# An attention and mixture-of-experts kernel: keys of unit 0 ahead of its diagonals on GpSimd, its state update behind its y, two decay tables turned one unit earlier

## The chip, the cores and the metric

The kernel runs on one core of a Trainium2 chip. The metric is the device time of one execution in microseconds (us); smaller is better. The engines are TensorE (PE; its weight loads are shown apart as PEld), VectorE (DVE), ScalarE (ACT), GpSimd (POOL) and SyncE (SP), which here only issues DMA transfers. Each engine works through its own instructions in program order.

## The reference

An attention with a decaying state feeds two dense blocks. For batch b, head h and step t, with r, k, v of width 48 and per-head vectors w (decay) and u (bonus):

```
y[t]  = r[t] @ (state + outer(u * k[t], v[t]))
state = w * state + outer(k[t], v[t])
```

There are 4 batches, 8 heads and 768 steps, all in fp32. The y of all heads, laid out as 3072 tokens of 384 features, goes through a soft mixture of 8 experts with 4 slots each (a softmax over tokens to fill the slots, a two-layer expert, a softmax over slots to mix back), and then through a two-layer block of width 2048 with a leaky relu.

## The kernel before, in words

The attention works in 24 units: 6 chunks of 128 steps, and in each chunk 4 pairs of heads. Unit i belongs to chunk i // 4 and pair i % 4, and holds all 4 batches. Its data come in two transfers: rk (r and k with the features on the partitions, 512 KB) and tk (v, k and r with the steps on the partitions, 576 KB). Both have 5 buffers, so tk of unit i+5 can be fetched only when unit i has read its own for the last time. All transfers are issued on SP, in program order (load, L225).

For one unit, the steps and the engines they run on are:

- powers (L285): a table of powers of w for a pair, from scans on DVE, with copies on ACT. It is done once per pair, for the first four units only.
- powers_t (L293): turns that table with a PE transpose into PSUM (tile psE, pool psM, 2 buffers) and copies it on ACT into KH (L297).
- scale (L304): multiplies r and k of rk by the powers; the k half on DVE, the r half on POOL or, for units 3 to 6 and a few more, on DVE (L309).
- bonus (L311): r * u * k, two operations, on DVE for units 0 and 1 and on POOL after them (L315, L318).
- diag (L320): sums that product on DVE into Dg (L323) and spreads it into the diagonal of the tile base: on POOL by an affine_select for units 0 and 1 (L329), on ACT by 8 operations for the others (L338). base has 2 buffers.
- keys (L343): multiplies k of tk in place by KH, on POOL (L348).
- scores (L354): 8 products on PE of k and r into the PSUM tile A (L359), which has one buffer.
- keep (L364): copies the causal half of A over base, two operations on DVE (L367). It frees A for the scores of the next unit.
- attend (L375): y of the unit on PE, from base and v (L398) and, from chunk 1 on, from the state (L390).
- update (L403): 8 products on PE of the keys and v into the PSUM tile U of pool psM (L412), and one operation on DVE that puts U into the state St (L418 in chunk 0, L420 after it).
- evac (L424): copies y to SBUF on ACT (L431); logits and tokens (L433, L445) take it on to the mixture.

The loop over units (L568) writes the order of the work on every engine out by hand: unit i+4 is loaded, unit i+2 scaled, unit i+1 scored and kept, unit i attended. The steps of the first units stand ahead of the loop, with dummy products on PE (warmup, FILL) between them. The state of chunk 0 is first read by the attend of unit 4, so the updates of units 0 and 1 need not stand directly behind their y: in this kernel the update of unit 0 is issued at the end of turn 1, that of unit 1 in the middle of turn 2 (between the scores and the keep of unit 3), and from unit 2 on each stands at the end of its own turn. keys(0) is issued in turn 0, keys(1) at the end of turn 0, keys(2) at the end of turn 1. The transposes of tables 2 and 3 both stand at the end of turn 1.

After the attention come the experts, then the mixing and the first products of the last block, and from about 164 us to the end the long loop of the last block (L1028, L971).

Of the kernel before, what the change touches and what calls it, by code (L numbers as in the profile page):

```python
# [118 lines left out]
def chunked(ctx, tc, rk, tok, wT, urep, phi, w1, w2, w2f, win, wout, outT, dbg=None, check=False):  # L119
# [35 lines left out]
    def load_w2_unit(j):  # L155
        t = ld.tile([128, 3 * DM], F32, name=f"w2t{j}", tag="tk")
        load_w2(t, 5 * j, 3)
        load_w2(rkf[(NU - NLD + j) % NLD].rearrange("p a b c -> p (a b c)"), 5 * j + 3, 2)
# [12 lines left out]
    def narrow_b(t, k, out=None):  # L171
        lo = t[:, k, 0]
        nc.vector.tensor_scalar(
            lo if out is None else out, lo.bitcast(U32), 2.0**-29, 7.0, op0=ALU.mult, op1=ALU.min
        )
# [117 lines left out]
    def powers_t(hp):  # L293
        e = ex[:, hp, :]
        ps = psM.tile([128, 128], F32, name=f"psE{hp}", tag="m")
        nc.tensor.transpose(ps[:, 0:R], e[:, C : 2 * C], ident[:R, :R])
        nc.scalar.copy(  # L297
            KH[:, hp, :].rearrange("p (h d) -> p h d", h=2),
            ps.rearrange("p (h d) -> p h d", h=2)[:, :, 0:D],
        )  # L300
# [3 lines left out]
    def scale(i, eng=nc.gpsimd, part=(0, 1)):  # L304
        for x in part:
            t = rk_t[i][:, x]
            e = ETp[:R] if (x or i in SCALE_V) and i else ET
            e = e[:, i % NP : i % NP + 1, :].broadcast_to([R, B, C])
            (nc.vector if x or i in SCALE_V else eng).tensor_tensor(t, t, e, op=ALU.mult)  # L309

    def bonus(i, eng=nc.gpsimd):  # L311
        hp = i % NP
        kk = tk_t[i][:, 1]
        rr = tk_t[i][:, 2]
        eng.tensor_tensor(  # L315
            rr, rr, u_sb[:, hp : hp + 1, :].broadcast_to([128, B, 2 * D]), op=ALU.mult
        )
        eng.tensor_tensor(rr, rr, kk, op=ALU.mult)  # L318

    def diag(i):  # L320
        rr = tk_t[i][:, 2]
        Dg[i] = sm.tile([128, 2 * B], F32, name=f"Dg{i}", tag="Dg")
        nc.vector.tensor_reduce(  # L323
            Dg[i].rearrange("p (h b) -> p b h", h=2),
            rr.rearrange("p b (h d) -> p b h d", h=2), op=ALU.add, axis=AX.X,
        )
        base[i] = bp.tile([128, 2, B, C], F32, name=f"base{i}", tag="base")
        if i in AFFINE:
            nc.gpsimd.affine_select(  # L329
                out=base[i].rearrange("p a b c -> p (a b) c"),  # L330
                in_=Dg[i].unsqueeze(2).broadcast_to([128, 2 * B, C]),
                compare_op=ALU.is_equal, fill=0.0,
                base=-(C - 1), pattern=[[0, 2 * B], [1, C]], channel_multiplier=1,
            )
            return
        for b in range(B):
            for h in range(2):
                nc.scalar.activation(  # L338
                    base[i][:, h, b, :], anti, AF.Copy, scale=Dg[i][:, h * B + b : h * B + b + 1]
                )  # L340


    def keys(i, eng=nc.gpsimd):  # L343
        if i >= NU - NP:
            return
        hp = i % NP
        kk = tk_t[i][:, 1]
        eng.tensor_tensor(  # L348
            kk, kk, KH[:, hp : hp + 1, :].broadcast_to([128, B, 2 * D]), op=ALU.mult
        )  # L350
# [3 lines left out]
    def scores(i):  # L354
        a = apsum[i] = psA.tile([128, 2, B, C], F32, name=f"A{i}", tag="A")
        for b in range(B):
            for h in range(2):
                p0 = 64 * h
                nc.tensor.matmul(  # L359
                    a[:, h, b, :], rk_t[i][p0 : p0 + D, 1, b, :], rk_t[i][p0 : p0 + D, 0, b, :],  # L360
                    start=True, stop=True,
                )
# [40 lines left out]
    def update(i):  # L403
        c, hp = divmod(i, NP)
        if c < NC - 1:
            v = tk_t[i][:, 0]
            u = psM.tile([128, B, D], F32, name=f"U{i}", tag="m")
            kk = tk_t[i][:, 1]
            for b in range(B):
                for h in range(2):  # L410
                    n = D if h else 64
                    nc.tensor.matmul(  # L412
                        u[64 * h : 64 * h + n, b, :], kk[:, b, D * h : D * h + n],
                        v[:, b, D * h : D * h + D], start=True, stop=True,
                    )
            st = St[:, hp]
            if c == 0:
                nc.vector.tensor_copy(st, u[:R])  # L418
            else:
                nc.vector.scalar_tensor_tensor(  # L420
                    st, st, W128[:, hp : hp + 1], u[:R], op0=ALU.mult, op1=ALU.add
                )
# [114 lines left out]
    def load_weights(n):  # L537
        if n < WH:
            wirs[n] = wp.tile([128, WCW, 2], I32, name=f"wir{n}", tag="wt")
            load_wide(win[n], wirs[n])  # L540
        elif n < WH + 16:
            load_w1(n - WH)
        else:
            load_rows(n - WH - 16)
# [10 lines left out]
    powers(1)  # L555
    scale(0, nc.vector, part=(1, 0))
    bonus(0, nc.vector)
    diag(0)
    powers_t(0)
    scores(0)  # L560
    warmup(FILL[0])
    scale(1)
# [5 lines left out]
    for i in range(NU):  # L568
        c, k = divmod(i, NP)
        for n in range(len(WST)):  # L570
            if WST[n] == i:
                load_weights(n)
        if i + NLD - 1 < NU:
            load(i + NLD - 1)
        else:
            load_w2_unit(i + NLD - 1 - NU)
        if i + 2 < NU:
            scale(i + 2)
        for _ in range(FILL_L.get(i + 1, 0)):
            nc.tensor.matmul(  # L580
                lw[0].rearrange("p a t -> p (a t)")[:, C:], ident,
                u_sb.rearrange("p a d -> p (a d)"), start=False, stop=True, skip_group_check=True,
            )
        if i + 1 < NU:
            scores(i + 1)
            if i == 2:
                update(1)
            keep(i + 1)
        slot = bool(c) and k == 1
        if i >= 1 and not slot:  # L590
            logits(i - 1)
        if 2 <= i < NP:
            tokens(i - 2)(nc.scalar.copy)
        if i + 2 < NU:
            bonus(i + 2)
        if i == 0:
            keys(0)
        attend(i)
        if slot:
            soft2(c - 1)  # L600
        evac(i)
        if c and k == 0:
            soft1(c - 1)
        if i < 2:
            for hp in ((1,), (2, 3))[i]:
                powers_t(hp)
            keys(i + 1)
        if i == 0:
            powers(3)
        if i == 2:  # L610
            keys(3)
        if i == NP:
            nc.gpsimd.memset(ones, 1.0)
        if i == NU - 2:
            yps[NU - 1] = psE.tile([128, 4, C], F32, name="ylast", tag="E")
            nc.vector.memset(yps[NU - 1][32:64, 0:2], 0.0)
        if check and i == NU - 2:
            rc0 = ap.tile([R, NP], F32, name="rc0")
            nc.vector.tensor_single_scalar(rc0, w_sb, WLO, op=ALU.is_ge)
            nc.vector.scalar_tensor_tensor(rc0, w_sb, WHI, rc0, op0=ALU.is_le, op1=ALU.mult)  # L620
            nc.vector.tensor_reduce(mst[:R, 6:7], rc0, op=ALU.add, axis=AX.X)
            nc.vector.memset(mst[:R, 7:8], 1.0)
        if i + 2 < NU:
            diag(i + 2)
            if i + 2 >= NP:
                keys(i + 2)
        if i > 1:
            update(i)
        elif i == 1:
            update(0)  # L630
        if i >= NP - 1:
            tok_copy = tokens(i - 1)
        if slot:
            pS = slots(c - 1)
            logits(i - 1)
        if i >= NP - 1:
            tok_copy(nc.vector.tensor_copy if c and k == 0 else nc.scalar.copy)
        if slot:
            slots_add(c - 1, pS)
        if i in NARROW:  # L640
            j, x = divmod(NARROW.index(i), 2)
            w = slice(x * WCW // 2, (x + 1) * WCW // 2)
            low = psM.tile([128, WCW // 2], I32, name=f"low{i}", tag="m")
            narrow_b(wirs[j], w, low)
            narrow_c(wi[:, j, w], wirs[j], w, low)
            narrow_d(wi[:, j, w], wirs[j], w, low)
        if i in NARROW_A:
            j, x = divmod(NARROW.index(NARROW_A[i]), 2)
            w = slice(x * WCW // 2, (x + 1) * WCW // 2)
            narrow_a(wi[:, j, w], wirs[j], w)  # L650
# [557 lines left out]
```

## Time and profile before

| what | value |
|---|---|
| time, median of 3 runs | 387.8 us (386.18 to 390.62) |
| the profiled execution, its own time | 384.81 us |
| its span, first to last instruction | 383.1 us |
| mean granted TensorE clock | 0.994 |
| busy PE / DVE / ACT / POOL | 96% / 72% / 61% / 37% of the span |
| read from memory | 64.80 MB |

The shares are averages over stages with different limits. What the change touches lies in the first 30 us or so, where the first units start up; so the stretch of those units, engine by engine, is what has to be read. Times in the rows below are counted from the start of the span. A row of the timeline has the start, the duration, the engine, the line, the operation and, in brackets, how long the engine stood idle just before it and what ended that. Neighbours of one kind are merged, with their count behind an x.

### The profile page before, as it was taken

How to read it: one execution, taken by the hardware profiler on the slowest of the kernel's cores; microseconds unless marked ns; L12 is line 12 of the kernel's file. 1: busy time of each engine (PE TensorE's matmuls, PEld its weight loads, DVE VectorE, ACT ScalarE, POOL GpSimd, SP SyncE). 2: the span in 40 equal slices, each digit the busy share in tenths (PEclk: the TensorE clock that was granted, in tenths of full speed). 3: DMA queues.
4: the chain of work that ended last, by engine and by line, in shares of the span. 5: the costliest groups of instructions: out<-in, count | busy, mean ns of one | idle time of the engine just before them, and what ended most of it. 6: DMA issues, size and time to landing. Idle time of an engine off the chain costs nothing.

```text
span 383.1 us, 8324 instructions
## 1 busy us (share of the span) xinstructions
PE 366.6 (96%) x3160; PEld 283.1 (74%) x3160; DVE 274.7 (72%) x478; ACT 232.2 (61%) x541; POOL 141.7 (37%) x145
## 2 busy tenths in 40 slices
PE   6799999999989999899999999999999999999994
PEld 3478778788765346778888878888888888888883
DVE  6879998888986544877577755777766766586762
ACT  3379879888883133756775657677655455545540
POOL 4797889988614002155433312554200000000000
PEclk9899999999999999999999999999999999999999
DMA  7979999999999999300022220000000220021202
GB/s 244 395 266 417 415 415 414 416 418 411 417 418 407 420 426 421 154 2 0 0 86 82 83 84 0 1 2 1 2 2 0 82 84 0 1 99 67 82 3 90
DMA packets 18018, 70.16 MB, mean 183 GB/s; under 512 B 2240, under 2 KB 3248, under 8 KB 17840
## 3 DMA queue, kind: packets, MB, share of 16 engines
q1 hardware_dynamic: 17968, 69.53, 45.7%
q8 instruction: 27, 0.44, 0.5%
q14 instruction: 23, 0.19, 0.1%
HBM read 64.80 MB, written 4.72 MB: 181 GB/s over the span
## 4 chain that ended last, share of the span: by engine, by line
PE 85%; DVE 7%; ACT 3%; DMA 2%; issue 2%; SPq 1%; DVEq 0%; ACTq 0%
PE o L1028 49%; PE h L971 5%; PE A L359 5%; PE Y L398 5%; PE po L806 3%; PE ph L763 3%; PE Y L390 2%; PE U L412 2%; PE px L448 2%; DMA tk<-in_tok_dram 2%; PE l L440 2%; DVE base L367 2%; PE l L517 1%; DVE rkb L309 1%; DVE t L981 1%
## 5 line engine op out<-in xcount | busy, mean ns | idle before, releaser
L985 ACT CAST gh<-t 128x512 fp32r<-128x512 f32 x94 | 58.4, 621 | 70.4 <-DVE t L981 67.8
L981 DVE TENSOR_TENSOR t<-t,h 128x512 f32<-128x512 f32 (+1 forms) x97 | 65.6, 677 | 23.9 <-ACT t L977 23.2
L1028 PE MATMUL o<-gh,woh 128*128 128x512 f32 x279 | 80.1, 393 | 0.2 <-ACT woh L873 0.2
L1028 PE MATMUL o<-gl,woh 128*128 128x512 f32 x279 | 79.9, 392 | 0.0
L1028 PE MATMUL o<-gh,wol 128*128 128x512 f32 x279 | 79.8, 392 | 0.0
L990 DVE TENSOR_TENSOR gl<-t,gh 128x512 fp32r<-128x512 f32 x71 | 50.8, 715 | 39.8 <-ACT gh L985 39.8
L977 ACT ACTIVATE t<-h 128x512 f32<-128x512 f32 (+1 forms) x97 | 57.4, 593 | 10.2 <-PE h L971 10.1
L1028 PEld LDWEIGHTS o<-gh,woh 128*128 128x128 f32 x279 | 52.2, 188 | 12.2 <-ACT woh L873 0.7
L1028 PEld LDWEIGHTS o<-gh,wol 128*128 128x128 f32 x279 | 52.1, 188 | 12.0 <-issue 0.4
L1028 PEld LDWEIGHTS o<-gl,woh 128*128 128x128 f32 x279 | 52.4, 188 | 11.5
L338 ACT ACTIVATE base<-anti,Dg 128x128 f32<-128x128 f32 x176 | 53.9, 391 | 5.4 <-DVE Dg L323 5.3
L990 POOL TENSOR_TENSOR gl<-t,gh 128x512 fp32r<-128x512 f32 x23 | 34.5, 1498 | 58.5 <-ACT gh L985 47.0
L971 PE MATMUL h<-cT,Gs 128*128 128x512 f32 (+1 forms) x97 | 37.3, 390 | 1.4 <-ACT Gs L939 1.4
L367 DVE COPY_PREDICATED base<-mask,A 128x512 f32<-128x512 int32 x48 | 34.1, 734 | 5.1 <-ACT base L338 4.5
L359 PE MATMUL A<-rkb 48*128 48x128 f32 x384 | 28.2, 286 | 4.1 <-DVE ETw L275 1.7
L359 PEld LDWEIGHTS A<-rkb 48*128 48x128 f32 x384 | 23.7, 188 | 9.4 <-POOL rkb L309 1.9
L398 PE MATMUL Y<-base,tk 128*48 128x128 f32 x376 | 26.4, 284 | 0.0
L315 POOL TENSOR_TENSOR tk<-tk,u_sb 128x384 f32<-128x384 f32 x22 | 22.1, 1004 | 7.8 <-DMA tk<-in_tok_dram 6.1
L398 PEld LDWEIGHTS Y<-base,tk 128*48 128x48 f32 x376 | 20.1, 126 | 5.1 <-issue 3.0
L318 POOL TENSOR_TENSOR tk<-tk 128x384 f32<-128x384 f32 x22 | 22.2, 1008 | 1.7
L971 PEld LDWEIGHTS h<-cT,Gs 128*128 128x128 f32 x97 | 18.0, 188 | 5.7 <-ACT Gs L939 1.8
L309 DVE TENSOR_TENSOR rkb<-rkb,ETp 112x512 f32<-112x512 f32 x31 | 20.4, 680 | 1.2 <-DMA rkb<-in_rk_dram 0.7
(198 smaller groups left out, 467.8 us busy)
## 6 DMA issues: line engine op xcount, KB each, us to landing
tk<-in_tok_dram SPq DMA_DIRECT2D x23, 576.0 KB, 9.3
rkb<-in_rk_dram SPq DMA_DIRECT2D x24, 512.0 KB, 9.5
w<-in_w_dram SPq DMA_DIRECT2D x16, 768.0 KB, 11.2
wir<-in_win_dram SPq DMA_DIRECT2D x8, 768.0 KB, 13.2
w<-in_w2f_dram SPq DMA_DIRECT2D x8, 768.0 KB, 12.7
out_dram<-sum SPq DMA_DIRECT2D x17, 256.0 KB, 2.1
wor<-in_wout_dram SPq DMA_DIRECT2D x4, 768.0 KB, 14.7
wir<-in_wout_dram SPq DMA_DIRECT2D x4, 768.0 KB, 4.3
```

Source lines behind the costliest of these rows:

```text
L309: (nc.vector if x or i in SCALE_V else eng).tensor_tensor(t, t, e, op=ALU.mult)
L318: eng.tensor_tensor(rr, rr, kk, op=ALU.mult)
L338: nc.scalar.activation(base[i][:, h, b, :], anti, AF.Copy, scale=Dg[i][:, h * B + b : h * B + b + 1])
L359: nc.tensor.matmul(a[:, h, b, :], rk_t[i][p0 : p0 + D, 1, b, :], rk_t[i][p0 : p0 + D, 0, b, :], start=True, stop=True,)
L367: nc.vector.copy_predicated(base[i][:, :, 2 * j : 2 * j + 2, :], mask.unsqueeze(1).unsqueeze(1).broadcast_to([128, 2, 2, C]), a[:, :, 2 * ...
L398: nc.tensor.matmul(ys[r][g : g + D, j, :], v[:, b, D * h : D * h + D], base[i][:, h, b, :], start=c == 0, stop=True, skip_group_check=True,)
L971: nc.tensor.matmul(t, Gs[f // 8][:, f % 8 * 128 : f % 8 * 128 + 128], cT[blk // 3][:, blk % 3 * TB + c.start : blk % 3 * TB + c.stop], sta ...
L977: nc.scalar.mul(tt[n][:, c], t, 0.01)
L981: nc.vector.tensor_tensor(tt[n][:, c], tt[n][:, c], h, op=ALU.max)
L985: nc.scalar.copy(gh[n][:, c], tt[n][:, c])
L990: eng.tensor_tensor(gl[n][:, c], tt[n][:, c], gh[n][:, c].bitcast(F32), op=ALU.subtract)
L1028: nc.tensor.matmul(os[m][:, c], w[j][:, k, m * 128 : (m + 1) * 128], g[n][:, c], start=k == 0 and w is woh and g is gh and c.start == 0, s ...
```

## The change

keys(0), with powers_t(0) that it needs, moves from turn 0 of the loop to just ahead of diag(0); on POOL it then comes before the affine_select of unit 0 instead of behind the bonus of unit 2. Every update stands at the end of its own turn: that of unit 0 in turn 0, ahead of the scores of unit 2, that of unit 1 in turn 1, ahead of the scores of unit 3. The transpose of table 2 moves from turn 1 to turn 0. No operation is added or taken away.

```diff
     bonus(0, nc.vector)
+    powers_t(0)
+    keys(0)
     diag(0)
-    powers_t(0)
     scores(0)
...
         if i + 1 < NU:
             scores(i + 1)
-            if i == 2:
-                update(1)
             keep(i + 1)
...
-        if i == 0:
-            keys(0)
         attend(i)
...
         if i < 2:
-            for hp in ((1,), (2, 3))[i]:
+            for hp in ((1, 2), (3,))[i]:
                 powers_t(hp)
             keys(i + 1)
...
-        if i > 1:
-            update(i)
-        elif i == 1:
-            update(0)
+        update(i)
```

## Rows read from the trace of the kernel before

**Rows 1.** The page, chain that ended last, shares of the span by engine.
```profile
PE 85%; DVE 7%; ACT 3%; DMA 2%; issue 2%; SPq 1%; DVEq 0%; ACTq 0%
```

**Rows 2.** Chain of waits, 16 to 26 us: start, us, what.
```profile
16.20 1.46 PE A L359 x16
17.66 0.58 PE l L440 x8
18.24 1.88 PE Y L398 x16
20.12 0.46 PE psE L296 x2
20.58 0.42 issue
21.00 0.64 PE U L412 x14
...
22.48 1.09 PE A L359 x16
23.57 0.59 PE U L412 x14
24.17 0.36 PE l L440 x8
...
25.06 1.01 PE Y L398 x16
```

**Rows 3.** Busy time by stretch: window, length, engines, granted clock, DMA share, GB/s.
```profile
17.00:18.00 1.00, 1.00 (x15) 0.56 (x12) 0.92 (x2) 0.74 (x4) 1.00 (x3) 0.50 1.05 421
...
20.00:21.00 1.00, 0.58 (x4) 0.32 (x3) 0.73 (x1) 0.95 (x4) 0.99 (x2) 0.83 0.12 45
...
42.00:53.00 11.00, 10.15 (x191) 8.47 (x189) 10.46 (x22) 8.36 (x25) 8.77 (x10) 1.00 1.02 412
```

**Rows 4.** Timeline of PE, scores of units 1 and 2.
```profile
11.01 1.16 PE L359 MATMUL A<-rkb 48*128 48x128 f32 x16 [0.86 <-DVE base L367]
...
16.20 1.46 PE L359 MATMUL A<-rkb 48*128 48x128 f32 x16 [1.71 <-DVE ETw L275]
```

**Rows 5.** Timeline of ACT, 7 to 33 us.
```profile
7.18 0.24 ACT L297 COPY KH<-psE 128x96 f32<-128x96 f32 x1 [1.25 <-PE psE L296]
...
14.77 0.24 ACT L297 COPY KH<-psE 128x96 f32<-128x96 f32 x1
...
17.67 2.45 ACT L338 ACTIVATE base<-anti,Dg 128x128 f32<-128x128 f32 x8 [0.26 <-DVE Dg L323]
...
21.64 2.45 ACT L338 ACTIVATE base<-anti,Dg 128x128 f32<-128x128 f32 x8 [0.60 <-DVE Dg L323]
...
26.60 2.45 ACT L338 ACTIVATE base<-anti,Dg 128x128 f32<-128x128 f32 x8
...
30.34 2.45 ACT L338 ACTIVATE base<-anti,Dg 128x128 f32<-128x128 f32 x8
```

**Rows 6.** Timeline of DVE, 9 to 25 us.
```profile
9.43 1.32 DVE L367 COPY_PREDICATED base<-mask,A 128x512 f32<-128x512 int32 x2
11.06 0.56 DVE L315 TENSOR_TENSOR tk<-tk,u_sb 128x384 f32<-128x384 f32 x1 [0.31 <-DMA tk<-in_tok_dram]
...
20.15 0.73 DVE L367 COPY_PREDICATED base<-mask,A 128x512 f32<-128x512 int32 x1 [0.43 <-ACT base L338]
21.05 0.55 DVE L323 TENSOR_REDUCE Dg<-tk 128x8 f32<-128x384 f32 x1 [0.16 <-POOL tk L318]
...
24.22 0.36 DVE L418 COPY St<-U 112x192 f32<-112x192 f32 x1 [0.98 <-PE U L412]
```

**Rows 7.** Timeline of POOL, affine_select of unit 0; keys of units 0 and 1.
```profile
8.22 1.09 POOL L329 TENSOR_SCALAR_AFFINE_SELECT base<-Dg 128x1024 f32<-128x1024 f32 x1 [4.71 <-DVE Dg L323]
...
17.01 1.96 POOL L348 TENSOR_TENSOR tk<-tk,KH 128x384 f32<-128x384 f32 x2
```

**Rows 8.** Timeline of SP, the transfer tk of unit 5.
```profile
21.73 0.33 SPq L238 DMA_DIRECT2D tk<-in_tok_dram  x1
```

## The prediction

> **What bounds the kernel now.** I read the chain that ended last first: PE carries 85% of it [rows 1], and from 16.2 us on it is PE nearly without a break. No PE work is added or removed, so the change can only win what PE loses by waiting or by its clock while the first units start up. The chain of waits between 16 and 26 us [rows 2] shows what that is. PE stands 1.71 us idle before the scores of unit 2 at 16.20 us, which wait for the keep of unit 1 on DVE [rows 4]. After that the granted clock is 0.50 (1.2 GHz) from 17 us on and full again within 20 to 21 us [rows 3]. In that stretch scores, logits and attend take 1.46, 0.58 and 1.88 us where the same work takes 1.09, 0.36 and 1.01 us a few us later [rows 2]: 0.37 + 0.22 + 0.87 = 1.46 us are lost to the clock. Behind them stand two transposes (0.46 us), a wait of 0.42 us and the update of unit 0 (0.64 us), all at the end of turn 1, and the update of unit 1 (0.59 us) in turn 2.
>
> A second loop runs beside PE: ACT spreads the diagonals of a unit (2.45 us), DVE keeps the second half (0.73 us), reduces the next unit's diagonal (0.55 us), and ACT spreads again [rows 5, 6]. With the handovers that is about 3.75 us, and the spreads of units 4 and 5 already follow each other at 30.34 - 26.60 = 3.74 us [rows 5]. Between 42 and 53 us DVE is busy 10.46 of 11 us [rows 3]: there DVE is the bound, and what is won earlier survives only if DVE's own queue has come forward.
>
> **The change part by part.** All times are those of the profiled execution: span 383.1 us, time 384.81 us, so 1.71 us lie around the span. The median of the runs shown is 387.8 us, 2.99 us above it; I carry the difference over unchanged.
>
> *keys(0) ahead of the diagonals of unit 0, on POOL.* It needs KH of pair 0, ready at 7.18 + 0.24 = 7.42 us [rows 5], so it starts at about 7.55 us (an estimate) and takes half of the pair's 1.96 us, 0.98 us [rows 7]. Queued behind it on POOL is the affine_select of unit 0, which moves from 8.22 us to 8.55 us, 0.33 us later, and behind that the r half of scale(1). The keep of unit 0 waits for the affine_select and moves from 9.43 to 9.76 us, ending at 11.08 us instead of 10.75 us. The next DVE step, the bonus of unit 1, had stood 0.31 us idle for its transfer until 11.06 us [rows 6]; that idle time covers all but 0.02 us. If the transfer landed earlier the cover is gone and the cost is 0.33 us. I take 0.05 us. On PE the scores of unit 1 move from 11.01 to about 11.34 us; that is hidden, since PE idles before the scores of unit 2.
>
> *keys(0) gone from 17 us.* POOL runs without a pause there, so the bonus of unit 3 ends 0.98 us earlier, and the 0.16 us that DVE waits for it at 21.05 us go [rows 6, 7]. Next late is DVE itself, with the second half of the keep of unit 2.
>
> *Table 2 and update(0) in turn 0.* Both fall into the 1.71 us in which PE stood idle. The transpose costs 0.46 / 2 = 0.23 us at the low clock. update(0) takes the PSUM buffer of table 1, so it waits for that copy on ACT, which ended at 14.77 + 0.24 = 15.01 us [rows 5] and now ends near 15.34 us; with some 0.1 us of handover and 0.64 us of work [rows 2] it ends near 16.1 us. Queued behind it are the scores of unit 2, due at 16.20 us, so it costs nothing by 0.1 us; at worst, if the copy comes later, I give it 0.3 us. The state copy of unit 0 (0.36 us [rows 6]) goes in front of scale(3) on DVE, where the 0.43 us wait before the keep at 20.15 us [rows 6] covers it; uncovered it would cost 0.36 us.
>
> *What that takes out of turns 1 and 2.* On PE: one transpose, 0.23 us, the wait, 0.42 us, and one update, 0.59 us, together 1.24 us, whatever the clock does. If the clock stays full, another 1.46 us; PE alone could then be 2.7 us ahead at the scores of unit 4. On DVE, the state copy of unit 1 at 24.22 us had waited 0.98 us for PE with the keep of unit 3 queued behind it [rows 6]. After the change that copy comes before scale(4), and the keep of unit 3 starts as soon as its diagonals are spread.
>
> *The sum.* The ACT-DVE loop then decides. Its entry hardly moves: the spread of unit 2 at 17.67 us waits for POOL's bonus of unit 2, which lies behind the affine_select of unit 1 and is not brought forward. So the spread of unit 2 ends at 20.12 + 0.05 us, the keep's second half at about 20.95 us, the reduction of unit 3 at 21.45 us, and the spread of unit 3 starts at 21.50 us instead of 21.64 us [rows 5]. One loop of 3.75 us later the spread of unit 4 starts at 25.25 us instead of 26.60 us. From there the old kernel also went at 3.74 us per unit, so the lead is kept: 1.35 us. PE is not later than that: at full clock its scores of unit 3 come when the keep of unit 2 has freed A, near 21.2 us, against 22.48 us.
>
> *The tk transfer of unit 5.* Its buffer comes free with update(0), so SP issues it near 16.2 us instead of 21.73 us [rows 8], and the four or so issues queued behind it follow. The DMA share had dropped to 0.12 at 20 to 21 us [rows 3]; that pause of some 2.4 us goes. Transfers of one queue stay in order, so none is delayed; POOL issues no transfers, so keys(0) holds none up. I cost this at nothing, because PE never waits for a transfer in the chain; its bound as a gain is the pause, 2.4 us.
>
> **Forecast: 1.3 us less** (1.35 less what the bounds of the hidden terms may eat): 383.5 us for a profiled execution, 386.5 us beside the median of 387.8 us. Chance 0.58.
>
> **Rivals.**
>
> *The clock falls all the same.* For it: the gap is not filled by long work, the update's products are short. Then PE decides: the scores of unit 2 start at 16.25 us and, at the old 1.46 + 0.58 + 1.88 us, one transpose, one update and the 0.84 us of dummy products between the end of the update, 21.64 us, and 22.48 us [rows 2], the scores of unit 3 start near 21.85 us instead of 22.48 us; with update(1) gone behind them, PE is 1.2 us ahead at unit 4, and ACT, which must first copy y of unit 2, about 1.1 us. 386.7 us; chance 0.14. The Trainium skill ("TensorE: Matmul & The Clock Gate", "HAM oscillation") has it that PE's clock drops after idle gaps longer than the 1.71 us seen here. By that rule the old gap did not cause the drop and filling it would not cure it, which is this rival; the trace, where the clock is at 0.50 within a us after this gap [rows 3, 4], speaks against it.
>
> *The transfers set the pace after all.* If the units past 30 us are limited by when their tk lands, the lead is that of the DMA queue, 2.4 us: 385.4 us. For it: the DMA share is 1.02 at 42 to 53 us; against it: in that stretch DVE has only half a us free [rows 3]. Chance 0.10.
>
> *The lead is given back.* Where DVE is the bound it gains only if its own queue starts earlier; if the keep of unit 5 is held by something that I hold to be early, the time is 387.8 us. Against it: the loop of ACT and DVE itself comes forward. Chance 0.10.
>
> *Slower: the clock falls one gap earlier.* keys(0) widens PE's gap before the scores of unit 1 from 0.86 to about 1.2 us [rows 4]. If the clock drops there, the dummy products and attend of unit 0 take double, some 2 us more, and update(0), now in front of the scores of unit 2, pushes these from 16.2 to about 17.8 us. If the clock is then low through attend of unit 1 as well, as before, nothing comes back from the clock, and of the 1.6 us only the 1.24 us that leave turns 1 and 2 return: 0.4 us slower, 388.2 us. It decides only if a gap of 1.2 us is enough; the one of 0.86 us was not, that of 1.71 us was. Chance 0.08.
>
> **How the numbers follow.** The prediction is the likeliest case, 386.5 us. The cases reach from 2.7 us less (PE alone) to 0.4 us more, 385.1 to 388.2 us; the three runs shown lie up to 2.8 us from their median, which adds about 1 us below and 0.6 us above for where a new median falls. Range 384.0 to 388.8 us. About 1%, 3.9 us, is what a measurement here can tell from no change. No case reaches it on either side, so same has 0.90; what is left is for run-to-run spread and for terms I don't see, 0.06 faster and 0.04 slower.
>
> **What would show it.** In the changed kernel's profile: keys(0) on POOL near 7.6 us with the affine_select at 8.5 us; the update of unit 0 on PE before 16.2 us, and the idle time before the scores of unit 2 below 0.6 us; the granted clock at full between 17 and 20 us; no DVE wait for U near 24 us; the spread of unit 4 starting near 25.25 us, and the whole rest 1.3 us earlier; tk of unit 5 issued near 16.2 us. The forecast is wrong if the spread of unit 4 has moved by clearly less or more than that, if the clock is low after a gap near 11 us, or if the lead at 30 us is no longer there at 60 us.

## The result and the profile after

The changed kernel takes 384.78 us (median of 14 runs, 383.43 to 385.42), the kernel before 387.78 us in 14 runs beside it (385.99 to 390.62). The medians differ by 3.0 us (0.77%), where 1.3 us less was forecast; the ratio given with the runs is 0.9914 (0.86% less), with a 95% interval of 0.989 to 0.9938. The interval leaves out 1, so the gain is real, and it is inside the 1% that I called the same.

The two profiled executions show only a part of it. Their times are 384.81 us before and 383.98 us after, 0.8 us apart; the one of before was faster than every one of the 14 runs of its kernel. So two questions stand: did the steps go as forecast, and where do 3.0 us come from?

The page's chain by engine, which answers to [rows 1], says that PE carries less of it and the loop of ACT and DVE more:

```profile
PE 71%; DVE 13%; ACT 7%; issue 3%; DMA 2%; POOL 1%; SPq 1%; ACTq 0%; DVEq 0%; POOLq 0%
```

In the chain of waits from 17 us on (start, us, what), in place of [rows 2], the loop stands alone: ACT spreads, DVE keeps, DVE reduces, ACT spreads. No PE step is left between 18 and 27 us.

```profile
18.07 2.47 ACT base L338 x8
20.56 0.06 DVE base L367
20.62 0.56 issue
21.18 0.55 DVE Dg L323
21.75 2.47 ACT base L338 x8
...
25.52 2.47 ACT base L338 x8
...
29.27 2.47 ACT base L338 x8
...
120.21 7.86 PE ph L757 x72
```

The spreads of units 2, 3, 4 and 5 start at 18.07, 21.75, 25.52 and 29.27 us; before, those of units 4 and 5 started at 26.60 and 30.34 us [rows 5]. Unit 4 was forecast for 25.25 us. At the first matmul of `ph`, where the work of the units has ended, the lead is 121.55 - 120.21 = 1.34 us; the chain of the kernel before has there:

```profile
121.55 7.86 PE ph L763 x72
```

PE's timeline, for [rows 4], shows the update of unit 0 in turn 0, and the waits around it small (in brackets: idle time before, and its releaser):

```profile
11.57 1.16 PE L359 MATMUL A<-rkb 48*128 48x128 f32 x16 [0.36 <-DVE base L367]
...
15.63 0.67 PE L412 MATMUL U<-tk 128*64 128x48 f32 x16 [0.49 <-ACT KH L297]
16.45 1.16 PE L359 MATMUL A<-rkb 48*128 48x128 f32 x16
...
21.39 1.16 PE L359 MATMUL A<-rkb 48*128 48x128 f32 x16 [0.73 <-issue]
```

POOL, DVE and SP, for [rows 6 to 8]: the keys of unit 0 stand ahead of the affine_select, the state copy of unit 1 waits for nobody, and tk of unit 5 is issued 5.34 us earlier.

```profile
7.89 1.00 POOL L348 TENSOR_TENSOR tk<-tk,KH 128x384 f32<-128x384 f32 x1 [4.37 <-ACT KH L297]
8.84 1.10 POOL L329 TENSOR_SCALAR_AFFINE_SELECT base<-Dg 128x1024 f32<-128x1024 f32 x1
...
11.44 0.56 DVE L315 TENSOR_TENSOR tk<-tk,u_sb 128x384 f32<-128x384 f32 x1
...
21.64 0.35 DVE L418 COPY St<-U 112x192 f32<-112x192 f32 x1
...
16.39 0.33 SPq L238 DMA_DIRECT2D tk<-in_tok_dram  x1
```

And the stretches of [rows 3] (window, length, busy time of PE, PEld, DVE, ACT, POOL, then granted clock, DMA share, GB/s): the clock is full at 17 us, the pause of the transfers at 20 us is gone, and between 42 and 53 us DVE is the busiest, as before.

```profile
17.00:18.00 1.00, 1.00 (x22) 0.68 (x20) 0.61 (x3) 0.70 (x3) 1.00 (x2) 1.00 1.00 406
20.00:21.00 1.00, 0.66 (x2) 0.04 (x1) 0.58 (x2) 1.00 (x4) 1.00 (x2) 1.00 1.00 396
42.00:53.00 11.00, 10.15 (x188) 8.23 (x186) 10.62 (x23) 8.69 (x29) 10.15 (x10) 1.00 1.02 413
```

**Runs by their granted clock.** Each run is listed with the mean clock that TensorE was granted over its span. The kernel before has 98 runs with their clock listed, on three chips (those beside the experiments, and before_again); the changed kernel has 26 (the 14 above, and after_again):

| mean granted clock | before: runs, median us | changed: runs, median us |
|---|---|---|
| 0.995 and more | 25, 386.13 | 25, 384.86 |
| 0.984 to 0.994 | 53, 388.5 | 1, 385.45 |
| 0.983 and less | 20, 390.7 | none |

Three in four runs of the old kernel lose clock, and only one in 26 of the new one; in the first row the two differ by 1.27 us. This table sorts runs by something that was not set; the experiments change the waits that the clock may follow from. The mean does not say where in the span the clock was lost.

### The profile page after: what moved, and what is told of

The parts are those of the page before. It is cut to its first block, busy times and chain, and to the rows that moved or that the text cites. A ratio compares the mean times of both kernels' runs of the same rounds, so it can differ in the third digit from the quotient of the medians.

```text
span 382.3 us, 8325 instructions
## 1 busy us (share of the span) xinstructions
PE 366.7 (96%) x3160; PEld 282.9 (74%) x3160; DVE 273.9 (72%) x478; ACT 232.3 (61%) x541; POOL 141.9 (37%) x145
## 4 chain that ended last, share of the span: by engine, by line
PE 71%; DVE 13%; ACT 7%; issue 3%; DMA 2%; POOL 1%; SPq 1%; ACTq 0%; DVEq 0%; POOLq 0%
PE o L1022 43%; PE h L965 5%; ACT base L338 4%; PE A L359 3%; PE Y L398 3%; PE po L800 3%; PE ph L757 3%; DVE t L975 2%; DMA tk<-in_tok_dram 2%; PE Y L390 2%; DVE base L367 2%; DVE gl L984 2%; PE px L448 2%; PE U L412 1%; DVE Dg L323 1%
## 5 line engine op out<-in xcount | busy, mean ns | idle before, releaser
L398 PE MATMUL Y<-base,tk 128*48 128x128 f32 x376 | 25.5, 277 | 0.0
L348 POOL TENSOR_TENSOR tk<-tk,KH 128x384 f32<-128x384 f32 x20 | 20.0, 1003 | 5.5 <-ACT KH L297 4.4
```

The costliest lines, as they stand in the source:

```text
L398: nc.tensor.matmul(ys[r][g : g + D, j, :], v[:, b, D * h : D * h + D], base[i][:, h, b, :], start=c == 0, stop=True, skip_group_check=True,)
```

## The experiments

Theories. **Order** (the forecast): the update of unit 0 and the transposes in turn 0 let the ACT-DVE loop start its rounds earlier; about 1.3 us, and the clock in [rows 3] is a part of that story. **Clock**: most of the 3.0 us is clock that typical executions of the old kernel lose, and the profile shown lost little of it. **Transfers**: the early transfers are what pays. The medians of the kernel before on the three chips used were 388.85, 387.69 and 387.91 us; each experiment is compared with those of its own chip. The changed kernel itself was run on the third chip only, and beside the 14 runs of the result; where an experiment on the first or second chip is set against it, that is across chips. In the runs at 0.995 and more, the kernel before has medians of 386.11, 386.14 and 385.96 us on the three.

### First chip: before 388.85 us (29 runs)

**before_again**, the old kernel unchanged, for a second profiled execution.

> The kernel before, once more, for its clock over several runs. The profile shown beforehand (384.81 us) is faster than all 14 timed runs (385.99 to 390.62 us), so the 3.0 us between the medians is 1.7 us more than the 1.3 us by which the changed profile leads at 120 us. Theory 'clock': the old gap before the scores of unit 2 makes the clock fall for longer, or in more places, in other executions than in the profiled one; then the runs here show mean granted clocks of 0.98 to 0.994, and the slower the run the lower its clock, about 1 us of time for each 0.005 of clock. Theory 'late stage': the clocks are like those of the changed kernel (0.995 to 0.999) and the spread comes from waits after 120 us; then time and clock do not go together.

388.33 us (12 runs), ratio 0.9983 [0.9946, 1.002]; mean clock 0.980 to 0.996. Its profiled execution took 387.9 us, near the medians of the kernel before, and is another story from [rows 2 to 4]. The first gap of PE is there (1.42 us), but the clock stays up; PE comes early to the update of unit 0 and stands 1.77 us, where [rows 2] have 0.42 us. Then the clock falls. PE's timeline:

```profile
15.80 1.16 PE L359 MATMUL A<-rkb 48*128 48x128 f32 x16 [1.42 <-DVE ETw L275]
...
20.44 0.64 PE L412 MATMUL U<-tk 128*64 128x48 f32 x16 [1.77 <-POOL tk L315]
...
22.36 2.08 PE L359 MATMUL A<-rkb 48*128 48x128 f32 x16
```

ACT in the same stretch, and then busy time of a window:

```profile
17.28 2.46 ACT L338 ACTIVATE base<-anti,Dg 128x128 f32<-128x128 f32 x8 [0.26 <-DVE Dg L323]
...
20.11 0.37 ACT L297 COPY KH<-psE 128x96 f32<-128x96 f32 x2
```

```profile
22.00:28.00 6.00, 6.00 (x55) 4.66 (x56) 2.72 (x6) 2.18 (x7) 5.76 (x7) 0.50 0.95 341
```

The update takes a PSUM buffer that the `KH` copies of tables 2 and 3 empty, and these stand on ACT behind the whole spread of unit 2; the update starts while they run (20.11 to 20.48 us). The releaser in brackets, POOL, is inferred; table2_only and keys0_only below speak against it. After that wait the scores take 2.08 us instead of 1.16 us, and the clock is 0.50 from 22 to 28 us. In the profile shown earlier the clock had already fallen at the first gap; PE came late, and so the second wait looked small.

What it costs is seen at the loop: here the spread of unit 4 starts at 29.09 us, against 26.60 us in [rows 5].

```profile
29.09 2.46 ACT L338 ACTIVATE base<-anti,Dg 128x128 f32<-128x128 f32 x8
```

**fill_gap**, the old kernel with dummy products in the first gap (the tile that they write to was widened for them, which is not shown here).

```diff
...
+            for _ in range(0 if i else 2):
+                nc.tensor.matmul(zp[:, 128:512], zz[:, 0:128], zz[:, 0:384], start=True, stop=True)
             keys(i + 1)
```

> The kernel before with two dummy products (384 columns each, 0.84 us) on PE in the 1.71 us gap before the scores of unit 2, written to PSUM columns that nothing reads; no step is moved. Theory 'clock': the granted clock stays full at 17 to 20 us, scores, logits and attend take 1.09, 0.36 and 1.01 us again, PE is up to 1.4 us earlier at the scores of unit 3, and most of the measured 3.0 us comes: 385 to 386 us. Theory 'order': the work taken out of turns 1 and 2 decides; ACT's spread of unit 4 still waits for U of unit 1 and the transposes, so 1.0 us at most, 386.8 us or more.

388.78 us (12 runs), ratio 0.9999 [0.9966, 1.0032]; clock 0.983 to 0.999, eight of twelve under 0.995. The first gap is closed, the second is not:

```profile
16.11 1.16 PE L359 MATMUL A<-rkb 48*128 48x128 f32 x16 [0.31 <-POOL tk L315]
...
20.74 0.64 PE L412 MATMUL U<-tk 128*64 128x48 f32 x16 [1.76 <-POOL tk L315]
```

```profile
22.00:28.00 6.00, 6.00 (x57) 4.86 (x58) 3.02 (x6) 2.47 (x8) 5.76 (x7) 0.51 0.90 331
```

Closing the gap that the prediction looked at is worth nothing by itself. One thing here does not fit *clock*: the four runs at 0.997 and more have a median of 387.97 us, although little clock is missing in them. No trace shows them, so the cause stays open.

**upd0_only**, the changed kernel with its tables and the update of unit 1 back where they were.

```diff
             scores(i + 1)
+            if i == 2:
+                update(1)
             keep(i + 1)
...
-            for hp in ((1, 2), (3,))[i]:
+            for hp in ((1,), (2, 3))[i]:
...
-        update(i)
+        if i != 1:
+            update(i)
```

> Of the change only keys(0) ahead and the update of unit 0 in turn 0; table 2 is turned in turn 1 and the update of unit 1 stands in turn 2 as before. Theory 'clock': the update alone cuts the gap to below 1.1 us, the clock stays up, and 2 of the 3 us come: 385.5 to 386 us. Theory 'order' (ACT-DVE loop): the keep of unit 3 still stands behind the state copy of unit 1, which waits for PE after the scores of unit 3, so the spread of unit 4 starts about 0.6 us later than in the changed kernel, near 26.1 us: 387 us.

385.03 us (6 runs), ratio 0.9897 [0.9848, 0.9945]; clock 0.993 to 1.0. The time is that of the changed kernel, on another chip, and the loop is as early as in the changed kernel: the spread of unit 4 starts at 25.30 us, against the 26.1 us that I gave to *order*. No update stands in turn 1 any more, so nothing there waits behind the spread.

```profile
16.52 0.67 PE L412 MATMUL U<-tk 128*64 128x48 f32 x16
```

```profile
25.30 2.45 ACT L338 ACTIVATE base<-anti,Dg 128x128 f32<-128x128 f32 x8
```

**keys0_only**, the old kernel with only the keys of unit 0 moved.

```diff
-    diag(0)
     powers_t(0)
+    keys(0)
+    diag(0)
...
-        if i == 0:
-            keys(0)
```

> Of the change only keys(0) ahead of the diagonals of unit 0; both updates and table 2 stay. Both theories: PE's gap before the scores of unit 2 stays near 1.2 us (the scores of unit 1 and attend come 0.4 us later), the clock falls as before, nothing of the lead comes: 387.5 to 388.2 us. If the wider gap before the scores of unit 1 brought the clock down earlier (the slower rival), the clock would be 0.50 somewhere between 11 and 16 us and the time above 388.2 us.

388.53 us (12 runs), ratio 0.9987 [0.9948, 1.0026]; clock 0.979 to 0.997. No gain by itself, and no harm: behind the gap before the scores of unit 1 the clock is full (1.00 at 14 to 16 us). The wait in turn 1 and the low clock behind it stay.

```profile
22.00:28.00 6.00, 6.00 (x60) 4.64 (x60) 3.24 (x7) 2.44 (x8) 5.76 (x6) 0.56 0.86 318
```

```profile
20.93 0.67 PE L412 MATMUL U<-tk 128*64 128x48 f32 x16 [1.72 <-ACT KH L297]
```

The keys of unit 0 are early here and the wait is as long, so they are not what the update waits for; here the bracket names ACT's copy.

### Second chip: before 387.69 us (35 runs)

**table2_only**, the old kernel with only table 2 turned in turn 0.

```diff
-            for hp in ((1,), (2, 3))[i]:
+            for hp in ((1, 2), (3,))[i]:
```

> The kernel before with table 2 turned in turn 0, nothing else moved. The update of unit 0 stays at the end of turn 1, but the PSUM buffer it takes is then free long before, so it no longer waits for the copies that stand on ACT behind the spread of unit 2. Theory 'second gap' (what the old kernel mostly loses is this wait, 1.77 us near 18.7 us in the second profile of the old kernel, and the low clock from 21.4 to 28 us that follows it): the wait goes, the clock is full at 22 to 28 us, and 2 to 3 us of the 3.0 us come: 385.5 to 387 us. Theory 'early update' (it takes the update of unit 0 in turn 0, with its earlier transfer): nothing or little comes, 388 us or more.

385.72 us (12 runs), ratio 0.9948 [0.9916, 0.9979]: 1.97 us less from one number in a tuple. Clock 0.991 to 0.998. With one transpose fewer in turn 1 the update of unit 0, still in turn 1 and with the keys of unit 0 where they were, finds its buffer free; the first gap of PE is still 1.07 us, and the clock is full behind it. The spread of unit 4 starts at 25.06 us, no later than in the changed kernel. Nine runs are at 0.995 and more, with a median of 385.73 us, only 0.41 us under those of the kernel before at that clock on this chip (386.14 us): most of the 1.97 us goes with the clock. (Of the two tables in the heading only this one is turned in an earlier turn; that of pair 0 is only moved ahead of diag(0), before the loop.)

```profile
15.86 1.16 PE L359 MATMUL A<-rkb 48*128 48x128 f32 x16 [1.07 <-DVE ETw L275]
...
18.56 0.67 PE L412 MATMUL U<-tk 128*64 128x48 f32 x16
```

```profile
20.00:24.00 4.00, 3.41 (x59) 2.86 (x60) 3.69 (x8) 3.08 (x11) 3.92 (x5) 1.00 0.79 244
```

**tk5_held**, the changed kernel with a one-element read of tk of unit 0 added, meant to keep that buffer busy so that tk of unit 5 goes out later.

```diff
         update(i)
+        if i == 1:
+            nc.vector.tensor_copy(hold, tk_t[0][0:1, 0, 0, 0:1])
```

> The changed kernel with one tiny DVE read (one element) of the tk tile of unit 0 at the end of turn 1, so that the transfer tk of unit 5 cannot be issued before about 21.8 us, as in the kernel before; the order on PE, ACT and POOL is that of the changed kernel. If the earlier transfers carry the gain ('transfers set the pace'), 1 us or more is lost: 386 us or more, and POOL waits for tk of unit 6 near 29 us. If PE's gaps and the clock carry it, the time stays within 0.4 us of the changed kernel: 384.5 to 385.4 us.

385.78 us (12 runs), ratio 0.9941 [0.991, 0.9972]: 0.85 to 1.0 us slower than the changed kernel on the chips where that was run (384.93 and 384.78 us), though the intervals of the ratios overlap. The clock is 0.996 to 1.0 in all twelve, so this is not clock. The transfer went out 3.31 us later than in the changed kernel, at 19.70 us (I had meant 21.8 us): when the update of unit 1 ended on PE, and two us ahead of the added read. So it did not wait for the read itself; why it waited for that update was not followed up.

```profile
19.70 0.33 SPq L238 DMA_DIRECT2D tk<-in_tok_dram  x1
...
21.62 0.13 DVE L627 COPY hold<-tk 1x1 f32<-1x1 f32 x1
```

The spread of unit 4 is on time at 25.24 us, but then POOL stands 1.94 us before the bonus of unit 6. The bracket names DVE; tk of unit 6, issued at 21.91 us, took 8.2 us to land, until about 30.1 us. POOL in this run, and the same step in the changed kernel, which does not wait:

```profile
30.20 1.01 POOL L316 TENSOR_TENSOR tk<-tk,u_sb 128x384 f32<-128x384 f32 x1 [1.94 <-DVE rkb L310]
```

```profile
28.45 1.00 POOL L315 TENSOR_TENSOR tk<-tk,u_sb 128x384 f32<-128x384 f32 x1
```

The loop slips with it. From the spread of unit 4 to that of unit 9 it takes 48.02 - 25.24 = 22.78 us, and 47.14 - 25.52 = 21.62 us in the changed kernel:

```profile
25.24 2.45 ACT L339 ACTIVATE base<-anti,Dg 128x128 f32<-128x128 f32 x8 [0.42 <-DVE Dg L324]
...
48.02 2.45 ACT L339 ACTIVATE base<-anti,Dg 128x128 f32<-128x128 f32 x8 [1.31 <-DVE Dg L324]
```

```profile
47.14 2.46 ACT L338 ACTIVATE base<-anti,Dg 128x128 f32<-128x128 f32 x8 [1.03 <-DVE Dg L323]
```

Of the lead of 1.34 us at `ph` 0.41 us is left (121.55 - 121.14; the line below is from this run's chain), and of the 1.27 us in the first row of the table 0.36 us (386.14 - 385.78, on this chip).

```profile
121.14 7.86 PE ph L760 x72
```

**after_wait**, the changed kernel with a gap put back on PE at the same place: the logits of unit 1, which wait for ACT's copy behind the spread of unit 2, ahead of the update of unit 1.

```diff
-        if i >= 1 and not slot:
+        if i >= 1 and not slot and i != 2:
             logits(i - 1)
...
+        if i == 1:
+            logits(1)
         update(i)
```

> The changed kernel with the logits of unit 1 put in front of the update of unit 1 instead of behind the scores of unit 3: nothing is added, but PE must then wait near 19.2 us for the copy of y that ACT makes behind the spread of unit 2, about 1.8 us, the length of the wait in the old kernel. Theory 'second gap': the clock falls to 0.50 within about 2 us behind the gap and stays there for some us; the time rises by 2.5 to 4 us over the changed kernel, 387.3 to 389 us, as in the kernel before. Without the clock the order alone would cost at most 1.5 us (scores of unit 3 near 22.9 us instead of 21.39 us): 386.3 us or less, at a full clock.

387.53 us (12 runs, 384.32 to 388.86), ratio 0.999 [0.9958, 1.0023]: the gain over the kernel before is gone. Three runs at a clock of 0.997 to 0.999 have a median of 384.81 us, as the changed kernel has; nine at 0.987 to 0.994 have 387.72 us. One kernel, one gap, and 2.9 us between its runs by clock. In the profiled execution (385.79 us, clock 0.994) the clock held behind this gap and fell far later, at 154 us, as it did in that of upd0_only (0.993):

```profile
21.25 0.43 PE L440 MATMUL l<-xT,phi_sb 112*32 112x128 f32 x8 [1.82 <-ACT xT L431]
```

```profile
21.00:24.00 3.00, 2.75 (x42) 1.95 (x42) 2.48 (x5) 2.37 (x9) 2.92 (x4) 1.00 1.02 416
...
154.00:156.00 2.00, 2.00 (x7) 1.81 (x8) 1.92 (x4) 1.32 (x3) 0.00 (x0) 0.50 0.27 111
```

So no trace shows the fall behind this gap; that the slower of the other runs lose their clock there is argued from their number. Six of the twelve have 0.987 or 0.988, as the profiled executions of before_again, fill_gap and keys0_only have (0.987), and the changed kernel without the gap has none of 26.

**table2_fill**, table2_only and the dummy products of fill_gap together.

> The kernel before with table 2 turned in turn 0 and two dummy products in the gap before the scores of unit 2: both gaps of the old kernel closed, both updates and keys(0) at their old places. Theory 'second gap': no low clock before 100 us, time within 1 us of the changed kernel, 384.8 to 386 us; what is missing to it is the keep of unit 3 that still stands behind the state copy of unit 1. Theory 'early update': 387.5 us or more.

385.91 us (12 runs), ratio 0.9966 [0.9937, 0.9996], as table2_only without the filler. Nine runs at 0.995 and more have a median of 385.71 us. I expected no low clock before 100 us; the profiled execution (387.8 us, clock 0.987) has it, later: of the 2 us before 48 us PE is busy 0.96 us, it stands 1.16 us until 48.12 us, and the scores take 2.08 us again. The same gap leaves the clock full in tk5_held's profile: there PE is busy 0.84 of these 2 us, stands 1.16 us before the scores at 47.59 us, and these take 1.16 us.

```profile
48.12 2.08 PE L359 MATMUL A<-rkb 48*128 48x128 f32 x16 [1.16 <-issue]
```

```profile
46.00:48.00 2.00, 0.96 (x18) 0.63 (x13) 2.00 (x5) 1.24 (x3) 1.84 (x3) 1.00 1.01 418
...
50.00:52.00 2.00, 2.00 (x30) 1.13 (x30) 1.97 (x5) 1.36 (x5) 1.84 (x3) 0.50 1.07 422
```

### Third chip: before 387.91 us (22 runs)

**after_again**, the changed kernel unchanged.

> The changed kernel once more, beside its variants on one chip: 384.5 to 385.1 us, clock 0.995 to 0.999 in nearly all runs.

384.93 us (12 runs), ratio 0.9928 [0.9898, 0.9958]; clock 0.993 to 1.0. The result repeats. Its profiled execution (383.57 us) stands against that of before_again (387.9 us, on the first chip): 4.33 us, of which 29.09 - 25.12 = 3.97 us are there at the spread of unit 4.

```profile
25.12 2.45 ACT L338 ACTIVATE base<-anti,Dg 128x128 f32<-128x128 f32 x8 [0.42 <-DVE Dg L323]
```

**weights_later** and **weights_later2**, the changed kernel with weight transfers between the units' transfers put off, in two ways.

```diff
-WST = [*range(2, 8), *range(9, 14), *range(15, 19), 20, 20, 21, 21, 22, 22, NU]
+WST = [2, *range(4, 14), *range(15, 19), 20, 20, 21, 21, 22, 22, NU]
```

(weights_later2: `[2, 4, 5, 6, *range(8, 15), *range(15, 19), ...`.)

> The changed kernel with the weight transfers of turns 3 to 7 issued one turn later each (none in turn 3, one in turn 8), so that rk and tk of units 6 to 12 queue behind 0.77 MB less. If the transfers still hold units 7 to 12 in the changed kernel (POOL's wait of 1.36 us at 41.93 us), as holding tk of unit 5 back cost about 1 us, the stage up to the experts ends up to 0.7 us earlier than 120.14 us and the time falls to 384.2 us or less. If DVE is the bound there, the time stays within 0.3 us of the changed kernel. A loss of over 0.5 us would mean that the weights themselves come late for units 5 to 11.

> As the kernel with the weights one turn later, and from turn 7 on two turns later (none in turn 7 either, one in turn 14). Where transfers hold, a further 0.3 us at most; where they don't, the same as the changed kernel, 384.5 to 385.1 us.

384.67 us (9 runs), ratio 0.9916 [0.9881, 0.9952], and 384.60 us (8 runs), ratio 0.9909 [0.9872, 0.9946]. Both are the changed kernel's time on this chip (384.93 us): with the early tk these weight transfers do not hold the units up.

## Why the prediction was right, and where its sizes were off

**The number.** The median came out 1.7 us under the forecast of 386.5 us. It lies in the range of 384.0 to 388.8 us, but the range was that wide for the spread of three runs and for other cases, not for a term that I had seen; that it holds the result is in part luck.

**The loop of ACT and DVE decides, up to about 51 us: shown.** It is the chain of the changed kernel there, and unit 4's spread starts at 25.52 us where 25.25 us was forecast. Counted from the spread of unit 2 it comes after 7.45 us, where the forecast had 25.25 - 17.72 = 7.53 us and the kernel before 26.60 - 17.67 = 8.93 us. The lead at 120 us is 1.34 us where 1.35 us was forecast; that the two agree to 0.01 us is luck, for in after_again `ph` starts at 119.79 us, 0.42 us earlier. The steps on the way came close: the keys of unit 0 at 7.89 us (forecast 7.55), the affine_select at 8.84 us (8.55), U of unit 0 ending at 15.63 + 0.67 = 16.30 us (16.1), scores of unit 2 without a wait, scores of unit 3 at 21.39 us (21.2), tk of unit 5 issued at 16.39 us (16.2), no wait for U at the state copies.

**The covered cost, "I take 0.05 us", was right in its two cases.** The bonus of unit 1 started at 11.44 us instead of 11.06 us [rows 6] and the spread of unit 2 at 18.07 instead of 17.67 us [rows 5]; that looks like a cover that failed. But both chains of waits put the bonus down to the transfer of tk of unit 1, issued at 3.63 us, which took 7.71 us after and 7.34 us before:

```profile
3.63 7.71 DMA tk<-in_tok_dram
```

```profile
3.63 7.34 DMA tk<-in_tok_dram
```

So most of the 0.4 us is this execution's later transfer and not the moved keep, which ended at 9.97 + 1.34 = 11.31 us. Where the transfer lands earlier the keep does show: after_again starts this bonus at 11.09 us, before_again at 10.66 us, 0.43 us apart, near the 0.33 us that I gave for the cover gone. Over all profiled executions the spread of unit 2 starts at 17.28 to 17.67 us with keys(0) in its old place (five) and at 17.69 to 18.37 us with it moved (eight).

```profile
11.09 0.54 DVE L315 TENSOR_TENSOR tk<-tk,u_sb 128x384 f32<-128x384 f32 x1
```

**Mis-sized, first: "The median of the runs shown is 387.8 us, 2.99 us above it; I carry the difference over unchanged."** That difference was not a constant around the span. Most runs of the old kernel lose clock, the changed kernel's hardly any: 1.27 us of the 3.0 us stand between runs at 0.995 and more, which answers to the forecast's term, and the rest, about 1.7 us, goes with the clock. This split is an estimate from sorted runs, and the runs of fill_gap at a high clock show that not every slow run is one of low clock. The place is the wait of the update of unit 0 in turn 1. I priced it at 0.42 us from [rows 2], but that is one execution; in the profiled executions of before_again, fill_gap and keys0_only it is 1.72 to 1.77 us, with 0.50 to 0.56 of the clock for the 6 us after it. Taking that wait away alone brings the clock back (table2_only: nine of twelve runs at 0.995 and more, 11 of 35 for the kernel before beside it), closing the first gap alone does not (fill_gap), and with a gap put back at the same place nine of twelve runs are under 0.995 (after_wait).

**Mis-sized, second: the tk transfer of unit 5, "I cost this at nothing".** With its transfer 3.31 us later (19.70 instead of 16.39 us) the kernel is about 0.9 us slower at full clock, and 0.41 of the 1.34 us of lead is left at `ph` (one execution each; two of the changed kernel differ by 0.42 us there). So the 1.35 us do not come from the order of work on PE, DVE and ACT alone; they are kept only because the transfers come forward as well. The rival *transfers* was right that the pause counts, and wrong in its size: the lead is 1.34 us and not 2.4 us, and putting off the weight transfers won nothing more. I had looked for transfers in PE's waits only. POOL waits for them, and DVE's and ACT's loop waits for POOL; the trace of the kernel before had such a wait, in front of the bonus of unit 6:

```profile
30.32 1.00 POOL L315 TENSOR_TENSOR tk<-tk,u_sb 128x384 f32<-128x384 f32 x1 [1.24 <-DMA tk<-in_tok_dram]
```

**The rival that the clock falls all the same** is refuted for this change: 25 of 26 runs are at 0.995 or more. The rule named with it, that the clock drops after idle gaps longer than these (the Trainium skill, "TensorE: Matmul & The Clock Gate", "HAM oscillation"), does not cover what the traces show: in before_again the clock falls behind a gap of 1.77 us, in table2_fill behind one of 1.16 us. Nor does a gap of that size always do it: in after_wait's profiled execution 1.82 us left the clock full, in tk5_held's 1.16 us.

**The slower rival, the clock one gap earlier,** did not come true in either profiled execution of the changed kernel. In the profiled execution the gap before the scores of unit 1 became 0.36 us; in after_again it is 1.07 us, about the 1.2 us of the rival, and the clock is full behind it:

```profile
11.44 1.16 PE L359 MATMUL A<-rkb 48*128 48x128 f32 x16 [1.07 <-DVE base L367]
```

```profile
11.00:14.00 3.00, 2.56 (x26) 1.71 (x28) 2.44 (x7) 0.39 (x3) 1.12 (x2) 1.00 1.02 396
```

**The lead given back:** not before 120 us. Between the two profiled executions some 0.5 us of the 1.34 us are lost later, at 150 to 191 us, where the chain after passes through ACT and DVE; one pair of executions, not followed up, and the medians do not show it as a loss.

**What stays open.** The loss through a later tk was measured on one chip and is set against the changed kernel on another. Why a gap drops the clock in one execution and not in the next was not settled. Nor whether the parts add: upd0_only gains 3.8 us against 388.85 us on the first chip (6 runs), the changed kernel 3.0 us elsewhere, and the intervals overlap. Which piece of upd0_only does it, the update moved out of turn 1 or the state copy ahead, was not tried apart.

## What to carry to other kernels

Before a difference between a profile and its median is carried over, list the granted clock of several runs: the profiled execution may be the rare one, and the wait that looks small in it may be small only because another stall came first. Where several PE waits follow each other, ask what the next one becomes if the first closes, and take the cheapest move that shortens it; here one transpose one turn earlier gave 2.0 of the 3.0 us. Look for late transfers at every engine of the loop that decides, not at PE alone.

## What the runs showed of the hardware that was not expected

The granted clock fell behind PE gaps of 1.16 to 1.77 us, from full to 0.50, the lower of its two levels (1.2 of 2.4 GHz). It stayed there for about 3 us in [rows 3] and for 6 to 7 us in before_again, fill_gap, keys0_only (from about 22 us) and table2_fill (from 48 us), with small fp32 products at nearly twice their time (scores 2.08 us against 1.16 us). Gaps of 1.16 us (tk5_held) and 1.82 us (after_wait) left it full in other executions. In after_wait, on one chip, three runs kept a mean of 0.997 and more and nine did not. In the old kernel's 98 runs time and mean clock go together with a correlation of -0.90; from 0.995 and more to 0.983 and less the medians rise by 4.6 us. The first transfers did not land at the same time in every execution: tk of unit 1, issued at 3.63 us in both, took 7.34 us in the profiled execution before and 7.71 us in the one after.
